# A narrower first kv, fewer z matmuls and another order of copies in a polysketch attention and GELU kernel

## The chip, the cores and the metric

The kernel runs on one core of a Trainium2 chip. The metric is the device time of one execution in microseconds (us). Before the change it is 271.33 us, the median of three runs (270.78 to 271.49). The engines are named as in the profile: PE is TensorE (PEld its weight loads), DVE is VectorE, ACT is ScalarE, POOL is GpSimd, SP is SyncE, which here only starts transfers.

## The reference

Polynomial-sketch attention on 4 batches, 4 heads, 1088 tokens and 32 channels per head, then a two-layer MLP with the exact GELU on the 4352 rows of 128 channels:

```python
def phi(x):                                   # 32 channels -> 64 features
    a = np.einsum('rd,bhsd->bhsr', S1, x)
    b = np.einsum('rd,bhsd->bhsr', S2, x)
    return np.einsum('bhsi,bhsj->bhsij', a, b).reshape(*x.shape[:-1], r * r)
q_p, k_p = (phi(q), phi(k))
kv = np.einsum('bhsf,bhsd->bhfd', k_p, v)     # per head 64 x 32
z = np.sum(k_p, axis=2)                       # per head 64: the features summed over the tokens
num = np.einsum('bhsf,bhfd->bhsd', q_p, kv)
den = np.einsum('bhsf,bhf->bhs', q_p, z)[..., None] + 1e-06
x = num / den                                 # then (B, S, H*D)
h = x @ w_in                                  # 128 -> 2048
g = 0.5 * h * (1.0 + erf(h * inv_sqrt2))
out = g @ w_out                               # 2048 -> 128
```

## The kernel before

Each batch has 8 tokens on each of 128 partitions (the main part, 1024 tokens) and a rest of 64 tokens. Batch 0 is computed alone at the start; later batches' attention is woven into the MLP's products. Tiles that matter: `k_p` holds the main part's features (two tiles per batch, heads of equal parity together), `k_p_rem` those of the rest, `k_s` (the buffers `bits_r`) features added over tokens, `kz` the finished kv and z of a batch.

Batch 0: the features are the stationary operand and v, widened by 32 columns of ones, moves; kv comes out in columns 0 to 31 and z, repeated, in columns 32 to 63.

```python
def kv_first(ps, r, tokens=range(J)):
    for i in tokens:
        ch, t, one = i // 4, i // 2 % 2, i % 2
        for c in range(NP):                   # two heads side by side
            pe.matmul(ps[c * F:(c + 1) * F, r * 2 * D:(r + 1) * 2 * D], lhsT=flat(k_p[0, r][:, t, c * 4 + ch * 2 + one]),
                      rhs=v_aug[r][:, c, i, :], start=(r == 0 and i == 0), stop=False, skip_group_check=True)
# kv_first_rem: the same for the rest, with v_rem_aug[0]
```

Later batches: v or ones is the stationary operand and the features move, four heads side by side. The features of the main part are added over t and over half of what is left, so that two sums per head remain, which go through a product with ones:

```python
def add_tokens(b, r, eng):                    # cut: reshapes
    eng.tensor_add(out=k_s[r], in0=kp[:, 0], in1=kp[:, 1])
    eng.tensor_add(out=k_s[r][:, :, 0], in0=k_s[r][:, :, 0], in1=k_s[r][:, :, 1])

def kv_sum(b, ps):
    for i in range(J):
        ch, t, one = i % 2, i // 4, i // 2 % 2
        for h in range(H):
            kv_product(ps, main["v", b][:, h, i, :], flat(k_p[b, h % 2][:, t, h // 2 * 4 + ch * 2 + one]), b, h, 0, start=i == 0)
    for m in range(2):
        for h in range(H):
            kv_product(ps, ones, k_s[h % 2][:, h // 2, 0, m], b, h, 1)
    for part in range(2):
        for h in range(H):
            kv_product(ps, ones_rem[b // 2] if part else v_rem_aug[b][:, h, :], flat(k_p_rem[b % 2][:, h]), b, h, part, stop=True)
```

Batch 1's `add_tokens` runs on GpSimd, those of batches 2 and 3 on VectorE, right after the features. GpSimd's main work is `token_sums`, four adds or subtractions of 128x512 for each block of four hidden products.

The opening, in the order in which each engine works (cut):

```python
key_turn(0, 0, hidden_bank(), by_act)
keep_busy(1, bank, 128)                       # a product of zeros that fills a gap on TensorE
sketches()
# ... features of batch 0, expand_products(0), kv_first, kv_first_rem
query_turn(1, lambda **a: late.append(a))     # transposes; the copy is kept for later
act.copy(out=kz[0], in_=kv_bank[:, :128])
w_in[0].mantissas(); w_in[0].signs(); w_in[0].product(pool)   # weights from 64-bit words
# ...
w_in[1].low_words()
by_act(**late[0])
w_in[1].fields(); w_in[1].exponents(); w_in[1].mantissas()
for banks, tokens in zip(nd, parts):
    numerators_by_token(0, banks, tokens)
expand_products(1)
for banks, tokens in zip(nd, parts):
    divide(0, banks, tokens, by_head_pair=True)
expand_copy(1, 0)
turn_half(0, 0, hidden_bank(), by_dve)
turn_half(0, 1, hidden_bank(), by_act)
for half in range(2):
    first_hidden(half, range(1))
w_in[1].signs(); w_in[1].product(pool)
expand_copy(1, 1)
```

The instructions of an engine run in the order of the text; what a wait on one of them holds up, it holds up for everything behind it on that engine.

Of the kernel before, what the change touches and what calls it, by code (L numbers as in the profile page):

```python
# [8 lines left out]
FP = mybir.dt.float32  # L9
# [7 lines left out]
def kernel(  # L17
# [18 lines left out]
    pe, dve, act, pool, sp = nc.tensor, nc.vector, nc.scalar, nc.gpsimd, nc.sync  # L36
    B, H, S, D = q.shape
    R = S1.shape[0]
    F = R * R
# [37 lines left out]
    def hidden_bank():  # L77
        return hps.tile([128, CW], FP, name="h_ps")
# [146 lines left out]
    kz_late = big.tile([128, 128], FP, name="kz_late")  # L225

    def rearrange_kz():
        at = [x.rearrange("f (r two d) -> f r two d", r=2, two=2) for x in (kz_late, kz[0])]
        for c in range(NP):
            to, of = (x[c * F:(c + 1) * F] for x in at)  # L230
            for two in range(2):
                pool.tensor_copy(out=to[:, :, two], in_=of[:, :, two if c == 0 else 1 - two])

    ones = big.tile([128, D], FP, name="ones")

    ones_rem = [big.tile([128, D], FP, name=f"ones_rem{i}") for i in range(B // 2)]
    for i, t in enumerate(ones_rem):
        pool.memset(t, 0.0)
        pool.memset(t[i * REM:(i + 1) * REM], 1.0)

    v_rem_aug = [big.tile([128, H, D if b else 2 * D], FP, name=f"v_rem_aug{b}") for b in range(B)]
    pool.memset(v_rem_aug[0], 0.0)
# [2 lines left out]

    v_aug = [att.tile([128, NP, J, 2 * D], FP, name="sums") for r in range(2)]
    for t in v_aug:
        dve.memset(t, 1.0)

    class Rounding:  # L250

# [161 lines left out]
    def add_tokens(b, r, eng):  # L413

        words = mlp.tile([128, LC], U32, name="bits_r")
        k_s[r] = words.bitcast(FP).rearrange("p (c two one f) -> p c two one f", c=NP, two=2, one=2)
        kp = k_p[b, r].rearrange("p t (c two one) i j -> p t c two one (i j)", c=NP, two=2)
        eng.tensor_add(out=k_s[r].rearrange("p c two one f -> p (c two one f)"),
                       in0=kp[:, 0].rearrange("p c two one f -> p (c two one f)"),
                       in1=kp[:, 1].rearrange("p c two one f -> p (c two one f)"))  # L420
        eng.tensor_add(out=k_s[r][:, :, 0], in0=k_s[r][:, :, 0], in1=k_s[r][:, :, 1])

    def flat(features):
        return features.rearrange("p i j -> p (i j)")

    def kv_first(ps, r, tokens=range(J)):

        for i in tokens:

            ch, t, one = i // 4, i // 2 % 2, i % 2  # L430
            for c in range(NP):
                pe.matmul(ps[c * F:(c + 1) * F, r * 2 * D:(r + 1) * 2 * D], lhsT=flat(k_p[0, r][:, t, c * 4 + ch * 2 + one]),  # L432
                          rhs=v_aug[r][:, c, i, :], start=(r == 0 and i == 0), stop=False, skip_group_check=True)

    def kv_first_rem(ps):
        for r in range(2):
            for c in range(NP):
                pe.matmul(ps[c * F:(c + 1) * F, r * 2 * D:(r + 1) * 2 * D], lhsT=flat(k_p_rem[0][:, 2 * c + r]),
                          rhs=v_rem_aug[0][:, 2 * c + r, :], start=False, stop=True, skip_group_check=True)

    def kv_product(ps, lhsT, features, b, h, part, start=False, stop=False):

        at, c = kz_cols(b, h)[part], h // 2
        pe.matmul(ps[at:at + D, c * F:(c + 1) * F], lhsT=lhsT, rhs=features, start=start, stop=stop, skip_group_check=True)  # L444
# [5 lines that stand above are left out]
            for h in range(H):  # L450
                kv_product(ps, main["v", b][:, h, i, :], flat(k_p[b, h % 2][:, t, h // 2 * 4 + ch * 2 + one]), b, h, 0,
                           start=i == 0)
        for m in range(2):
            for h in range(H):
                kv_product(ps, ones, k_s[h % 2][:, h // 2, 0, m], b, h, 1)
        for part in range(2):
            for h in range(H):
                kv_product(ps, ones_rem[b // 2] if part else v_rem_aug[b][:, h, :], flat(k_p_rem[b % 2][:, h]), b, h, part,
                           stop=True)

    kv_T = {}

# [40 lines left out]
    def expand_copy(n, i):  # L503
        A[i] = att.tile([128, 2, CW // 2], FP, name="A_sb")
        act.copy(out=A[i][:, :, :width[n] // 2], in_=B_of[n, i][:, :, :width[n] // 2])  # L505
# [80 lines left out]
    def turn_half(n, i, ps, copy):  # L586
        if i == 0:
            xT[n] = att.tile([128, CW], FP, name="xT", bufs=3)
        for j in range(2):
            pe.transpose(ps[:, j * 128:(j + 1) * 128], in_=x_tok[n, i][:, j].rearrange("p h d -> p (h d)"), identity=ident)  # L590
        copy(out=xT[n][:, i * 256:(i + 1) * 256], in_=ps[:, :256])
# [26 lines left out]
    def first_hidden(half, fis):  # L618

        for fi in fis:  # L620
            if half == 0:
                first_banks[fi] = hidden_bank()
            cols = slice(half * 256, (half + 1) * 256)
            pe.matmul(first_banks[fi][:, cols], lhsT=w_tile(w_in_sb, fi), rhs=xT[0][:, cols], start=True, stop=True)  # L624
# [148 lines left out]
    def keep_busy(n, ps, cols=256):  # L773
        for i in range(n):
            noughts = [nc.const_aps.tensor(0.0, [128, m], FP) for m in (128, cols)]
            pe.matmul(ps[:, CW - cols:], lhsT=noughts[0], rhs=noughts[1], start=True, stop=True)  # L776
# [8 lines left out]
    r.signs()  # L785
    r.product_for_heads(SR_heads)
    key_turn(0, 0, hidden_bank(), by_act)
    keep_busy(1, bank, 128)
    sketches()
    key_turn(0, 1, hidden_bank(), by_act)  # L790
    query_turn(0)
# [19 lines left out]
    w_in[0].exponents()  # L811
    late = []
    query_turn(1, lambda **a: late.append(a))
    act.copy(out=kz[0], in_=kv_bank[:, :128])
    w_in[0].mantissas()
    w_in[0].signs()
    w_in[0].product(pool)
    load_w_out(0, gated=True)
    load_rest()
    w_out = [Rounding(w, beside=b) for w, b in zip(w_out_sb[:2], w_in)]  # L820
    w_in[1].low_words()
    by_act(**late[0])
    w_in[1].fields()
    w_in[1].exponents()
    w_in[1].mantissas()
    parts = [range(2), range(2, JC)]
    nd = [[hidden_bank(), hidden_bank()], [out_bank(), out_bank()]]
    for banks, tokens in zip(nd, parts):
# [1 line left out]
    expand_products(1)  # L830
    for banks, tokens in zip(nd, parts):
        divide(0, banks, tokens, by_head_pair=True)
    expand_copy(1, 0)
    turn_half(0, 0, hidden_bank(), by_dve)
    turn_half(0, 1, hidden_bank(), by_act)
    for half in range(2):
        first_hidden(half, range(1))
    w_in[1].signs()
    w_in[1].product(pool)
    expand_copy(1, 1)  # L840
# [9 lines left out]
    def at(t, f, *a):  # L850
        slots[t].append(lambda: f(*a))
# [19 lines left out]
    def outer_of_all(b, adds_by=dve):  # L871
        for r, a in enumerate(held["factors"]):
            k_p[b, r] = att.tile([128, 2, J, R, R], FP, name="k_p")
            for t in range(2):
                dve.tensor_mul(**spread(k_p[b, r][:, t], a[:, t, :, 0:R], factors(held["keys"][t], r)[:, :, R:2 * R]))
        for r in range(2):
            add_tokens(b, r, adds_by)

    held = {}

# [34 lines left out]
    at(18, expand_products, 2)  # L915
    at(18, query_features, 2, 0)
    at(19, query_features, 2, 1)
    at(21, finish_keys, 1)
    at(22, lambda: turn_kv(1, held["kv"]))
    at(23, query_turn, 3)  # L920
# [54 lines left out]
    for t in range(len(steps) + LAG):  # L975
        if t < 4:

            hidden(0, t)
            if t == 1:
                w_out[0].exponents()  # L980
                w_out[0].low_words()
                w_out[0].finish()
                w_out[1].fields()
            if t == 2:
                w_out[1].low_words()
            if t == 3:
                banks = work_banks()
                numerators_by_token(1, halves(banks), range(JC))
                w_out[1].mantissas(by_pool=True)
                w_out[1].exponents()  # L990
                divide(1, banks, range(JC), by_head_pair=False)
                w_out[1].signs()
                w_out[1].product()
                for u in range(4):
                    for f, *a in products[u]:
                        f(*a)
            continue
        if t == 4:
            for i, copy in enumerate((by_act, by_dve)):
                turn_half(1, i, work_bank(), copy)  # L1000
            for f, *a in products[t]:
                f(*a)
        for n in drains[t]:
            drain(n)
        if t < len(steps):
            n, fi = steps[t]
            hidden(n, fi, by_halves=t >= 18 and (n < NMAIN or fi < 5))
        if t < len(steps) and steps[t][0] < NMAIN and steps[t][1] % NB == NB - 1:
            n, b = steps[t][0], steps[t][1] // NB
            if b >= first_block(n):  # L1010
                token_sums(n, b)
        for f in slots[t]:
            f()
        for n in done[t]:
            store(n)
        if t != 4:
            for f, *a in products[t]:
                f(*a)
# [41 lines left out]
```

## Time and profile before

| | us | share of the span |
|---|---|---|
| time, median of three runs | 271.33 | |
| span of the profiled run | 269.7 | |
| PE busy | 264.9 | 98% |
| PEld busy | 138.8 | 51% |
| DVE busy | 154.3 | 57% |
| ACT busy | 136.6 | 51% |
| POOL busy | 170.2 | 63% |

Lines of the profile name the line of the kernel (L444), the engine, the tile written and the tiles read, the shape, and the count. Times in a timeline are the start and the length, both in us, and then the group. L432 and L438 are batch 0's kv, L444 the later batches' kv and z, L418 and L421 the two adds of `add_tokens`, L561 the numerators by token, L609 the hidden products, L659 to L662 the token sums on GpSimd. A busy PE is not a PE at its peak, since its matmuls overlap.

### The profile page before, as it was taken

The numbers are of one execution on the slowest core, as the hardware profiler recorded it, in microseconds if no ns is written. First come the engines' busy times: TensorE is split into PE (matmuls) and PEld (weight loads), VectorE is DVE, ScalarE is ACT, GpSimd is POOL, SyncE is SP. The second block draws the span as 40 slices with busy tenths as digits, with TensorE's granted clock in tenths as the row PEclk, the third lists the DMA queues.
The fourth block names the chain that finished last, engine by engine and source line by source line (L and its number), as shares of the span: only waits on it lengthen the run. The fifth ranks groups of instructions, "written<-read, shape, count | busy, mean of one in ns | idle before, by whom it ended". The sixth has DMA issues, their size and how long they took to land.

```text
span 269.7 us, 6251 instructions
## 1 busy us (share of the span) xinstructions
PE 264.9 (98%) x2559; PEld 138.8 (51%) x2559; DVE 154.3 (57%) x248; ACT 136.6 (51%) x272; POOL 170.2 (63%) x178
## 2 busy tenths in 40 slices
PE   8999999999999999999999999999999999999994
PEld 6745445354444545445445545444444444445794
DVE  5876878515793699379214996287018901750240
ACT  4664767456635633573347433663357334633431
POOL 3513007899998498468865896668866886777300
PEclk9999999999999999999999999999999999999999
DMA  6479263535201000110200000100200020011020
GB/s 203 125 223 351 56 171 67 160 69 163 47 2 29 12 0 2 23 20 0 41 1 2 0 2 17 24 2 5 36 0 0 2 40 2 0 22 20 1 42 20
DMA packets 37869, 13.52 MB, mean 50 GB/s; under 512 B 28240, under 2 KB 37200, under 8 KB 37840
## 3 DMA queue, kind: packets, MB, share of 16 engines
q1 hardware_dynamic: 37648, 13.05, 19.2%
q8 instruction: 20, 0.33, 0.5%
q10 hardware_dynamic: 192, 0.07, 0.1%
q14 instruction: 9, 0.07, 0.1%
HBM read 10.88 MB, written 2.23 MB: 49 GB/s over the span
## 4 chain that ended last, share of the span: by engine, by line
PE 95%; DVE 3%; ACT 1%; issue 0%; DVEq 0%; ACTq 0%
PE h_ps L609 43%; PE o_ps L694 32%; PE o_ps L745 5%; PE w_ps L498 3%; PE w_ps L742 3%; PE w_ps L538 3%; PE w_ps L444 2%; PE w_ps L776 1%; PE w_ps L375 1%; PE h_ps L333 1%; DVE x_tok L582 1%; DVE bits_m L287 1%; PE o_ps L432 0%; PE h_ps L624 0%; DVE bits_e L292 0%
## 5 line engine op out<-in xcount | busy, mean ns | idle before, releaser
L609 PE MATMUL h_ps<-xT,w_in 128*64 128x512 f32 (+3 forms) x516 | 139.8, 577 | 0.0
L616 ACT ACTIVATE block<-h_ps 128x512 f32<-128x512 f32 (+1 forms) x128 | 72.8, 571 | 101.6 <-PE h_ps L609 98.5
L694 PE MATMUL o_ps<-block,w_out 128*64 128x256 f32 x224 | 57.9, 381 | 0.0
L609 PEld LDWEIGHTS h_ps<-xT,w_in 128*64 128x64 f32 (+1 forms) x516 | 41.8, 143 | 28.6 <-issue 8.6
L659 POOL TENSOR_TENSOR bits_low<-block 128x512 f32<-128x512 f32 x28 | 36.4, 1302 | 27.7 <-ACT block L616 27.6
L694 PEld LDWEIGHTS o_ps<-block,w_out 128*64 128x64 f32 x224 | 30.0, 137 | 36.9 <-issue 27.4
L660 POOL TENSOR_TENSOR bits_a<-block 128x512 f32<-128x512 f32 x28 | 36.0, 1287 | 15.9 <-ACT block L616 15.6
L662 POOL TENSOR_TENSOR bits_m<-block,bits_e 128x512 f32<-128x512 f32 x28 | 36.4, 1298 | 2.2
L661 POOL TENSOR_TENSOR bits_e<-bits_a,block 128x512 f32<-128x512 f32 x28 | 36.2, 1294 | 2.2
L545 DVE RECIPROCAL den<-den 128x512 f32<-128x512 f32 (+1 forms) x7 | 21.9, 3121 | 13.6 <-ACT den L544 13.5
L694 PE MATMUL o_ps<-bits_a,small 128*64 128x256 f32 x112 | 29.0, 382 | 0.0
L694 PE MATMUL o_ps<-bits_m,w_out 128*64 128x256 f32 x112 | 28.8, 380 | 0.0
L694 PE MATMUL o_ps<-bits_low,small 128*64 128x256 f32 x112 | 28.7, 379 | 0.0
L694 PE MATMUL o_ps<-block,small 128*64 128x256 f32 x112 | 28.7, 379 | 0.0
L511 DVE TENSOR_TENSOR q_pT<-A_sb,w_ps 128x512 f32<-128x512 f32 x16 | 10.4, 682 | 30.4 <-ACT A_sb L505 30.3
L710 DVE TENSOR_TENSOR sums<-o_ps,sums 64x512 f32<-64x512 f32 x8 | 5.5, 683 | 35.9 <-ACT sums L707 20.4
L694 PEld LDWEIGHTS o_ps<-block,small 128*64 128x64 f32 x112 | 15.3, 137 | 18.0 <-issue 12.8
L549 DVE TENSOR_TENSOR xT<-w_ps,den 32x512 f32<-32x512 f32 (+1 forms) x28 | 18.2, 649 | 1.0
L694 PE MATMUL o_ps<-bits_e,small 128*64 128x256 f32 x112 | 16.8, 379 | 0.0
L745 PE MATMUL o_ps<-g,w_out 128*128 128x512 f32 x32 | 16.4, 600 | 0.2 <-DVE w_out L297 0.2
L544 ACT ACTIVATE den<-w_ps 32x512 f32<-32x512 f32 (+1 forms) x28 | 15.6, 557 | 1.3 <-PE w_ps L538 1.0
L694 PEld LDWEIGHTS o_ps<-bits_low,small 128*64 128x64 f32 x112 | 15.3, 137 | 0.0
(164 smaller groups left out, 318.5 us busy)
## 6 DMA issues: line engine op xcount, KB each, us to landing
block<-in_moe_w_in_dram SPq DMA_DIRECT2D x3, 512.0 KB, 7.0
block<-in_moe_w_out_dram SPq DMA_DIRECT2D x3, 512.0 KB, 10.2
k<-in_k_dram SPq DMA_DIRECT2D x48, 32.0 KB, 1.8
v<-in_v_dram SPq DMA_DIRECT2D x3, 512.0 KB, 4.3
q<-in_q_dram SPq DMA_DIRECT2D x24, 64.0 KB, 3.5
out_dram<-oT SPq DMA_DIRECT2D x24, 64.0 KB, 2.2
k<-in_k_dram SPq DMA_DIRECT2D x2, 256.0 KB, 2.8
q<-in_q_dram SPq DMA_DIRECT2D x2, 256.0 KB, 4.2
```

The lines of the kernel that those rows point to most:

```text
L511: dve.tensor_mul(out=qp[n].rearrange("f r (g x) -> f g r x", g=G)[:, 2 * i:2 * i + 2], in0=a, in1=b)
L544: act.activation(out=den[h * D:(h + 1) * D, :W], in_=banks[h // 2][at:at + D, :W], func=ACT.Copy, bias=1e-6)
L545: dve.reciprocal(out=den[:, :W], in_=den[:, :W])
L549: dve.tensor_mul(out=xT[n][rows, :W], in0=banks[h // 2][at:at + D, :W], in1=den[rows, :W])
L609: pe.matmul(ps[rows, :W], lhsT=w[:, rows], rhs=xT[n][:, :W], start=True, stop=True)
L616: act.activation(out=g_of[n, fi][:, :W], in_=ps[:, :W], func=ACT.Gelu)
L659: pool.tensor_sub(out=s[3], in0=a11, in1=a21)
L660: pool.tensor_add(out=s[1], in0=a21, in1=a22)
L661: pool.tensor_sub(out=s[2], in0=s[1], in1=a11)
L662: pool.tensor_sub(out=s[4], in0=a12, in1=s[2])
L694: pe.matmul(acc[n][bank][half * 64:(half + 1) * 64, col:col + HW], lhsT=fixed, rhs=moving, start=opens and e == 0 and name in "4715", stop ...
L745: pe.matmul(o_of[n], lhsT=w_tile(w_out_sb, fi), rhs=g, start=first, stop=final)
```

## The change

It makes batch 0's kv from v and a single column of ones (33 moving columns instead of 64), and spreads z only when it is rearranged for later use. For later batches it adds the features over all of a partition's main tokens and, on that batch's 64 partitions, over the rest as well, on VectorE: then one product with ones per head gives z, and the products of the rest with ones and the second half of the sums go away. In the opening it changes the order of some copies and weight steps behind the first numerators, and halves a filler product. The diff, cut to its core (the matching slices in `kv_first_rem` and the smaller memset of `v_aug` are as one expects):

```diff
     def rearrange_kz():
...
+            pool.tensor_copy(out=to[rows, :, c], in_=of[rows, :, 0])
+            pool.tensor_copy(out=to[rows, :, 1 - c], in_=of[rows, :, 1, 0:1].broadcast_to([F, 2, D]))
...
+    def add_last(b, eng):
+        rows = slice(b // 2 * REM, (b // 2 + 1) * REM)
+        for r in range(2):
+            to = k_s[r][:, :, 0, 0]
+            eng.tensor_add(out=to, in0=to, in1=k_s[r][:, :, 0, 1])
+            eng.tensor_add(out=to[rows], in0=to[rows], in1=k_p_rem[b % 2][rows, r::2].rearrange("p c i j -> p c (i j)"))
...
-                pe.matmul(ps[c * F:(c + 1) * F, r * 2 * D:(r + 1) * 2 * D], lhsT=flat(k_p[0, r][:, t, c * 4 + ch * 2 + one]),
-                          rhs=v_aug[r][:, c, i, :], start=(r == 0 and i == 0), stop=False, skip_group_check=True)
+                pe.matmul(ps[c * F:(c + 1) * F, r * 2 * D:r * 2 * D + C], lhsT=flat(k_p[0, r][:, t, c * 4 + ch * 2 + one]),
+                          rhs=v_aug[r][:, c, i, :C], start=(r == 0 and i == 0), stop=False, skip_group_check=True)
...
-        for m in range(2):
-            for h in range(H):
-                kv_product(ps, ones, k_s[h % 2][:, h // 2, 0, m], b, h, 1)
-        for part in range(2):
-            for h in range(H):
-                kv_product(ps, ones_rem[b // 2] if part else v_rem_aug[b][:, h, :], flat(k_p_rem[b % 2][:, h]), b, h, part,
-                           stop=True)
+        for h in range(H):
+            kv_product(ps, v_rem_aug[b][:, h, :], flat(k_p_rem[b % 2][:, h]), b, h, 0, stop=True)
+        for h in range(H):
+            kv_product(ps, ones, k_s[h % 2][:, h // 2, 0, 0], b, h, 1, stop=True)
...
-    keep_busy(1, bank, 128)
+    keep_busy(1, bank, 64)
...
-    act.copy(out=kz[0], in_=kv_bank[:, :128])
+    kz_of, kv_of = (x.rearrange("f (r x) -> f r x", r=2)[:, :, :C] for x in (kz[0], kv_bank[:, :128]))
+    act.copy(out=kz_of, in_=kv_of)
...
+    by_act(**late[0])
     w_in[1].low_words()
-    by_act(**late[0])
     w_in[1].fields()
     w_in[1].exponents()
-    w_in[1].mantissas()
...
-    expand_copy(1, 0)
-    turn_half(0, 0, hidden_bank(), by_dve)
-    turn_half(0, 1, hidden_bank(), by_act)
+    turn_half(0, 0, hidden_bank(), by_act)
+    turn_half(0, 1, hidden_bank(), by_dve)
     for half in range(2):
         first_hidden(half, range(1))
+    expand_copy(1, 0)
+    w_in[1].mantissas()
     w_in[1].signs()
...
+        if adds_by is dve:                    # end of outer_of_all, which makes a batch's features
+            add_last(b, dve)
...
+    at(20, add_last, 1, dve)
     at(21, finish_keys, 1)                    # kv_sum(1)
...
             if t == 1:
+                w_out[0].low_words()
                 w_out[0].exponents()
-                w_out[0].low_words()
```

## The prediction

> **What bounds the kernel now.** I read the chain of work that ended last on the page first, then the chain in order of time over the opening, then each engine's timeline where the change touches it. The page's chain and its first group:
>
> ```profile
> PE 95%; DVE 3%; ACT 1%; issue 0%; DVEq 0%; ACTq 0%
> ...
> L609 PE MATMUL h_ps<-xT,w_in 128*64 128x512 f32 (+3 forms) x516 | 139.8, 577 | 0.0
> ```
>
> TensorE sets the end: what it has to do after the opening, plus every wait in it, is the time. So a matmul taken out of the steady part counts in full, and so does any time for which TensorE is made to wait. The chain in order of time shows the last place at which TensorE waits for another engine:
>
> ```profile
> 22.62 0.41 DVE bits_e L292
> ...
> 23.13 0.44 DVE w_out L297
> 23.56 0.14 issue
> 23.70 1.10 PE o_ps L745 x2
> ```
>
> Ahead of 23.70 us VectorE and ScalarE share the path; behind it TensorE runs without a gap to the end. The change touches both parts.
>
> **How a small matmul is paced.** The TensorE timeline (start, length, group; a float32 matmul leaves two records, except a transpose):
>
> ```profile
> 10.73 1.15 PE L432 MATMUL o_ps<-sums,k_p 128*64 128x64 f32 x32
> 11.81 0.45 PE L438 MATMUL o_ps<-v_rem_aug,k_p_rem 128*64 128x64 f32 x8
> 12.20 0.66 PE L333 MATMUL o_ps<-ident,q 128*128 128x128 f32 x4
> ...
> 20.04 1.14 PE L561 MATMUL w_ps<-kz,q_pT 64*64 64x33 f32 x64
> 21.11 1.98 PE L745 MATMUL o_ps<-g,w_out 128*128 128x512 f32 x4
> ```
>
> I use starts only. L432 and L438 put two heads side by side in the array, so 32 records are 16 pairs of records and 8 are 4. From 10.73 to 11.81 is 1.08 us, from 11.81 to 12.20 is 0.39: twelve pairs are 0.69, 58 ns for a pair, with 0.15 per change of group. L561 runs four tiles at once: 64 records are 16 quads in 1.07 us, and less 0.15 that is again 58 ns. L432 moves 64 columns, L561 only 33; what they share is a stationary operand 64 columns wide.
>
> **What the Trainium skill says.** Its page "TensorE: Matmul & The Clock Gate", section "LDWEIGHTS (loading the stationary operand)", puts a weight load at the columns of the stationary operand divided by 1.2, in ns. For 64 that is an estimate of 53 ns, near the 58 seen in both groups: the trace agrees that the load paces them. The page "SBUF — State Buffer", section "Who interferes with whom", says that a VectorE instruction with two SBUF inputs and a GpSimd instruction that reads SBUF exclude each other, and that the loser waits for the winner's whole instruction. The trace agrees, and this decides my number:
>
> ```profile
> 98.45 1.27 POOL L661 TENSOR_TENSOR bits_e<-bits_a,block 128x512 f32<-128x512 f32 x1
> 98.92 1.35 DVE L418 TENSOR_TENSOR bits_r<-k_p 128x512 f32<-128x512 f32 x1
> ...
> 99.80 1.61 POOL L662 TENSOR_TENSOR bits_m<-block,bits_e 128x512 f32<-128x512 f32 x1
> ...
> 100.31 1.38 DVE L421 TENSOR_TENSOR bits_r<-bits_r 128x256 f32<-128x256 f32 x1
> ...
> 101.61 0.68 DVE L418 TENSOR_TENSOR bits_r<-k_p 128x512 f32<-128x512 f32 x1
> ...
> 102.32 1.38 DVE L421 TENSOR_TENSOR bits_r<-bits_r 128x256 f32<-128x256 f32 x1
> ...
> 103.55 1.29 POOL L660 TENSOR_TENSOR bits_a<-block 128x512 f32<-128x512 f32 x1
> 103.63 0.70 DVE L484 STREAM_TRANSPOSE qT<-q 128x512 f32<-128x512 f32 x1
> 104.05 0.94 PEld L444 LDWEIGHTS w_ps<-k_p,v 128*32 128x32 f32 x64 [0.81 <-DVE bits_r L421]
> ...
> 104.97 0.41 PE L444 MATMUL w_ps<-bits_r,ones 128*32 128x64 f32 x16
> ```
>
> This is batch 2's feature sum. An L418 add with no GpSimd instruction in its way takes 0.68 us; L421 has half its elements and takes 1.38 each time, because it starts inside a GpSimd instruction of 1.3 us and finishes 0.28 after it. The two engines take turns. And the sums are ready at 103.70 for matmuls that want them at 104.97: only 1.3 us of slack.
>
> **Part by part.**
> Batch 0's narrower kv: 36 matmuls go from 64 to 33 moving columns. Their stationary operand stays 64 wide, so by the pair pace above nothing is saved. If the columns set the pace, a pair of records would fall to 33/64 of 58 ns, 28 ns less, and the 36 pairs (72 records) would give 1.0 us.
> The filler before the sketches: half its columns. Its two records stand 0.21 us apart before the clock has risen; 0.1 to 0.2 goes, on the path. I take 0.2.
> Order behind the first numerators: VectorE's mantissa product (13.44, 0.43 long) leaves the place ahead of the first division, which can start about 0.3 earlier; but the first half's copy, now on ScalarE, starts only after the transpose at the end of the expansion, so about 0.1 of it reaches the first hidden product. Further on, the low words move ahead of the exponents (0.4 us on ScalarE); yet the division for the second chunk waits for its numerators, which TensorE's order holds (20.04 to 21.11). I pass on 0.1 and no more. Opening: −0.3 us.
> Fewer matmuls in later batches: 48 per batch become 40. Four heads run side by side, and the row of 16 records of the ones product, 55.21 to 55.43 in batch 1, is four quads: 56 ns each. Eight matmuls are 16 records, four quads, 0.22 us; three batches, −0.67 us.
> The new adds: per batch four more VectorE adds, two pairs, the second of each pair depending on the first. All have two SBUF inputs. Unhindered a pair is under 0.5 us (an estimate from L418's 0.68 for 512 elements). But they are the last thing before the ones product, which now comes last of the sum, and GpSimd is busy with token sums of 1.27 to 1.34 us, four in a row.
> Batch 2, in turns: GpSimd's L660 holds until 104.84; first add, done 105.05; L661 until 106.25; second add, 106.45; L662 until 107.66; third and fourth, 108.1. The ones product would be due at 105.08, after the main products (0.92) and the four of the rest (0.11). TensorE stands for 3.0 us.
> Batch 3: the previous L421 ends at 162.57, GpSimd's next starts at 162.68. The first add slips in, the other three each wait for one GpSimd instruction: 167.0 against 164.2 due. 2.8 us.
> Batch 1: the adds come behind L511 at 54.35; GpSimd starts a row of four at 54.40. One add before it, three behind one instruction each: 58.9 against 55.3. 3.6 us.
> Sum of the waits: 9.4 us. Nothing behind them can take it back, as TensorE has no other gap. 271.33 − 0.3 − 0.67 + 9.4 = 279.8 us.
>
> **The rivals.**
> (a) The adds fit in. The intention of the change: fewer matmuls, and VectorE, busy 57% of the span, takes the work. The share speaks for it; the slack of 1.3 us in batch 2 against four taking-turns adds speaks against it. It would make 270.4 us.
> (b) Half of the waiting. If an add that waits for nothing follows its predecessor before GpSimd gets its turn, one GpSimd instruction of about 1.3 us falls out of each batch: 9.4 − 3.9 = 5.5, that is 275.9 us. Against it: at 159.39 an L418 that followed an L421 without a wait still took 1.76 us behind GpSimd's L662.
> (c) The columns do set the pace in batch 0: 1.0 us less than any of these. L561's 58 ns with 33 columns speaks against it.
> (d) More waiting: in batch 1 the GpSimd row starts within 0.05 us of the first add; if it wins, one more turn, +1.3: 281.
>
> **Range and chances.** The centre is the turn-by-turn count, 279.8. The low end is rival (b), 275.9, the high end (d) with a little on top, 281.8. The 2% line above the time before is 276.8, so slower by over 2% needs about 6.4 us of waiting: two thirds of my count. I give 0.8 to slower, 0.19 to the same (rival (a) and the low part of (b)), 0.01 to faster.
>
> **What would show it.** Right: the ones product waiting for VectorE's new adds in the waits, some 3 us in each of three batches; adds of 1.3 us mean where their elements would take 0.2 to 0.3; L432's successor still at 58 ns for a pair; TensorE's steady part beginning near 23.4. Wrong: ones products directly behind the rest's products with no idle time (then (a)), or a batch 0 sum half as long (then (c)). It would be most wrong if an add this small passed between GpSimd instructions without taking turns, or if the adds stood earlier in VectorE's queue than the trace of before lets me place them.

## The result, and the profile after

The changed kernel takes 282.33 us, the median of six executions (280.53 to 282.6), against 271.1 us before (270.78 to 271.5): a ratio of 1.0395, with a 95% interval of 1.036 to 1.0429. It is slower by 11.2 us, where 8.5 were predicted, and the time lies half a microsecond above the predicted range.

The page of the changed kernel, in its order: busy time of the engines, the clock granted to TensorE in 40 slices of 7 us, the chain that ended last, the costliest group.

```profile
PE 267.5 (95%) x2511; PEld 139.1 (50%) x2511; DVE 159.8 (57%) x260; ACT 136.4 (49%) x272; POOL 169.4 (60%) x174
...
PEclk9999999979999999799999999999999999999999
...
PE 79%; DVE 15%; ACT 3%; DMA 2%; issue 1%; SPq 0%; DVEq 0%
...
L609 PE MATMUL h_ps<-xT,w_in 128*64 128x512 f32 (+3 forms) x516 | 142.4, 588 | 0.0
```

VectorE's share of the chain has gone from 3% to 15%, so TensorE now waits for it somewhere in the steady part. The group of the hidden products, which the change doesn't touch, has gone from 139.8 to 142.4 us for the same 516 records. And the clock row has two slices at 7, the ninth and the seventeenth, that is around 60 and 115 us. The last two are not among the prediction's signs.

The waits of the changed kernel between 23 and 270 us (engine, tile and line, what it waited for; microseconds in all, times, longest):

```profile
ACT kv_T L465 <- PE w_ps L447: 10.7, 3, 3.8
...
PE w_ps L447 <- DVE bits_r L424: 7.7, 5, 2.3
...
PEld w_ps L447 <- DVE bits_r L424: 5.3, 3, 2.5
```

TensorE's ones product (L447) waits for the second new add (L424), in three batches, as predicted. Batch 2 in order of time, all engines (start, length, engine and line; L423 is the first add of a pair, L424 the second, L659 to L662 are GpSimd's token sums in the MLP):

```profile
107.55 1.30 POOL L660 TENSOR_TENSOR bits_a<-block 128x512 f32<-128x512 f32 x1
107.64 1.37 DVE L423 TENSOR_TENSOR bits_r<-bits_r 128x128 f32<-128x128 f32 x1
...
108.05 1.10 PE L447 MATMUL w_ps<-k_p,v 128*32 128x64 f32 x64
...
108.93 1.26 POOL L661 TENSOR_TENSOR bits_e<-bits_a,block 128x512 f32<-128x512 f32 x1
108.97 0.29 PE L447 MATMUL w_ps<-k_p_rem,v_rem_aug 128*32 128x64 f32 x8
109.04 1.31 DVE L424 TENSOR_TENSOR bits_r<-bits_r,k_p_rem 64x128 f32<-64x128 f32 x1
110.28 1.26 POOL L662 TENSOR_TENSOR bits_m<-block,bits_e 128x512 f32<-128x512 f32 x1
110.38 1.31 DVE L423 TENSOR_TENSOR bits_r<-bits_r 128x128 f32<-128x128 f32 x1
...
110.40 0.30 PE L447 MATMUL w_ps<-bits_r,ones 128*32 128x64 f32 x2 [1.14 <-DVE bits_r L424]
111.72 0.29 DVE L424 TENSOR_TENSOR bits_r<-bits_r,k_p_rem 64x128 f32<-64x128 f32 x1
...
112.06 0.31 PE L447 MATMUL w_ps<-bits_r,ones 128*32 128x64 f32 x6 [1.37 <-DVE bits_r L424]
...
112.31 0.43 PE L694 MATMUL o_ps<-block,w_out 128*64 128x256 f32 x1
```

Three adds in a row begin some 0.1 us after a GpSimd instruction has begun and end 0.15 us after it has ended (107.64 + 1.37 = 109.01 for 107.55 + 1.30 = 108.85); the fourth meets none and takes 0.29. TensorE does its main products at 108.05 and those of the rest at 108.97, and then stands until 112.06, but for two of the eight records of the ones product at 110.40, for which the first pair of adds is enough. That is the turn-by-turn count of the prediction. What it lacks is what comes next. The same kernel in stretches around the waits of batches 1 and 2 (stretch and its length; busy time and instructions of PE, PEld, DVE, ACT and POOL; the granted clock; DMA share and GB/s):

```profile
54.40:58.30 3.90, 1.01 (x30) 0.63 (x20) 3.87 (x4) 0.10 (x1) 3.74 (x4) 1.00 0.22 48
58.30:61.70 3.40, 3.40 (x12) 1.16 (x10) 0.01 (x1) 0.91 (x3) 1.68 (x2) 0.50 0.31 70
61.70:65.10 3.40, 3.40 (x28) 1.28 (x26) 0.00 (x0) 1.19 (x2) 2.54 (x3) 1.00 0.74 196
108.90:112.90 4.00, 1.50 (x42) 0.93 (x32) 3.87 (x6) 0.27 (x1) 2.53 (x2) 1.00 0.01 4
112.90:116.30 3.40, 3.40 (x18) 1.63 (x16) 1.98 (x4) 0.75 (x2) 0.00 (x0) 0.50 0.04 8
116.30:119.70 3.40, 3.40 (x51) 1.68 (x50) 0.12 (x1) 1.33 (x3) 1.10 (x1) 1.00 0.23 36
```

The second row of each three is the new thing: TensorE is busy again for all of it, but at half the clock, and gets 12 matmuls done where the stretch after it does 28, and 18 where the stretch after it does 51 (the products aren't the same ones, but the direction is plain). The page "TensorE: Matmul & The Clock Gate" of the Trainium skill, section "What's actually happening", says that the clock falls to half after an idle window of about 3.4 us. The trace agrees on the half, 0.50, and each of the two lasts 3.41 us. At half the clock such a stretch does 1.7 us less work. TensorE wasn't wholly idle ahead of it, though.

How idle it was can be read. The clock of this trace changes at 3.67, 58.28, 61.70, 112.90 and 116.31 us, and these times lie 16, 1, 15 and 1 times 3.413 us apart. So they belong to a row of stretches of that length. The two stretches that end where the clock falls, and the two across which batch 3's wait lies (172.91 to 175.55):

```profile
54.87:58.28 3.41, 0.72 (x10) 0.52 (x12) 3.38 (x4) 0.09 (x1) 3.25 (x4) 1.00 0.20 45
...
109.49:112.90 3.41, 1.13 (x14) 0.73 (x16) 3.31 (x5) 0.27 (x1) 1.97 (x2) 1.00 0.02 5
...
170.92:174.34 3.42, 2.05 (x78) 1.16 (x74) 3.32 (x5) 0.75 (x2) 3.03 (x3) 1.00 0.00 0
174.34:177.75 3.41, 2.44 (x24) 1.43 (x26) 3.06 (x5) 0.47 (x2) 0.77 (x1) 1.00 0.00 0
```

The clock fell behind 0.72 and 1.13 us of work and did not fall behind 2.05 and 2.44. From the clock's rise to the end of the kernel, the traces of all thirteen kernels have no exception to this: it fell behind every stretch with up to 1.46 us of TensorE work (e10_alike_dependent, 109.68 to 113.09) and behind none with 1.69 or more (e1_adds_left_out, 263.29 to 266.71). Of these runs, e1 leaves the adds out and e10 changes one of them; both are described below. By this, batch 3's wait cost no clock because it lies across two stretches: within one it would have left at most 0.8 us of work there, an estimate from 3.41 less 2.64.

Where the stretches lie differs between executions. Two of the six of the changed kernel, 280.53 and 280.65 us, have a mean clock of 0.992 and 0.993 in place of 0.987, which fits one half-clock stretch and not two; they left no trace, and a third, 282.41 us at 0.992, doesn't fit.

**Where 10.9 us came from**, in the profiled executions (269.67 before, 280.56 after). The waits are measured as the start of the first product behind the sum, less the time at which it was due, which is the start of the sum plus the work in it:

| Part | Predicted | Measured |
|---|---|---|
| Opening, until the product with `w_out` at 23.70 before, 22.87 after | −0.3 | −0.83 |
| 8 fewer matmuls in each of three sums | −0.67 | −0.67 (worked out) |
| Wait in batch 1 (58.08 for 54.72) | 3.6 | 3.36 |
| Wait in batch 2 (112.31 for 109.31) | 3.0 | 3.00 |
| Wait in batch 3 (175.55 for 172.91) | 2.8 | 2.64 |
| Two stretches of 3.41 us at half the clock | none | +3.4 |
| Sum | +8.4 | +10.9 |

The value for the fewer matmuls is the worked-out one, and the sum of the rest leaves room for it; the others are read from the trace. A run below bears it out: in e7_two_adds batch 3's sum has 4 matmuls fewer and no wait, and takes 1.37 us (162.72 to 164.09) against 1.48 before (163.18 to 164.66).

### The profile page after: what moved, and what is told of

Its sections match the earlier page's. It is cut to its first block, busy times and chain, and to the rows that moved or that the text cites. A ratio compares the mean times of both kernels' runs of the same rounds, so it can differ in the third digit from the quotient of the medians.

```text
span 280.6 us, 6162 instructions
## 1 busy us (share of the span) xinstructions
PE 267.5 (95%) x2511; PEld 139.1 (50%) x2511; DVE 159.8 (57%) x260; ACT 136.4 (49%) x272; POOL 169.4 (60%) x174
## 3 DMA queue, kind: packets, MB, share of 16 engines
HBM read 10.88 MB, written 2.23 MB: 47 GB/s over the span
## 4 chain that ended last, share of the span: by engine, by line
PE 79%; DVE 15%; ACT 3%; DMA 2%; issue 1%; SPq 0%; DVEq 0%
PE h_ps L609 36%; PE o_ps L694 25%; PE o_ps L745 5%; PE w_ps L498 3%; PE w_ps L742 3%; DVE bits_r L424 2%; PE w_ps L538 2%; DVE den L545 2%; DVE bits_r L423 2%; DVE bits_r L416 2%; DVE xT L549 2%; DVE k_p L876 2%; ACT den L544 2%; DMA q<-in_q_dram 2%; DVE bits_r L413 2%; PE w_ps L370 1%
## 5 line engine op out<-in xcount | busy, mean ns | idle before, releaser
L609 PE MATMUL h_ps<-xT,w_in 128*64 128x512 f32 (+3 forms) x516 | 142.4, 588 | 0.0
L659 POOL TENSOR_TENSOR bits_low<-block 128x512 f32<-128x512 f32 x28 | 36.1, 1290 | 38.4 <-ACT block L616 38.3
L662 POOL TENSOR_TENSOR bits_m<-block,bits_e 128x512 f32<-128x512 f32 x28 | 36.2, 1291 | 2.2
```

The source lines that it names most:

```text
L609: pe.matmul(ps[rows, :W], lhsT=w[:, rows], rhs=xT[n][:, :W], start=True, stop=True)
L659: pool.tensor_sub(out=s[3], in0=a11, in1=a21)
L662: pool.tensor_sub(out=s[4], in0=a12, in1=s[2])
```

## The experiments

The theory: the loss is the new adds taking turns with GpSimd, plus the clock that falls behind the two longest of the waits. Rivals: the opening or the shorter filler lost something too; the clock fell for another reason; the adds are slow by themselves and not for GpSimd.

### The adds left out, and the adds alone

**e1_adds_left_out**: the changed kernel, with the sums of later batches as before (48 matmuls); the narrow kv, the order and the filler stay changed.

```diff
-        if adds_by is dve:
-            add_last(b, dve)
...
-    at(20, add_last, 1, dve)
 # kv_sum again with two ones products and ones_rem
```

> The changed kernel with the later batches' sums as before (two ones products of the main part and the one of the rest, no new adds); batch 0's narrow kv and the new order stay. Theory (the new adds take turns with GpSimd and hold TensorE, and the clock falls in the holes): no waits in the three sums, clock 1.00, 269.9 to 270.9 us, that is the opening's gain of some 0.3 to 0.8 alone. Rival (the opening's order or the rearranged kz cost time as well): above 272 us.

Measured: 270.81 us (270.31 to 272.56), before 270.95; ratio 1.0002 [0.9987, 1.0018]. No wait for the new adds and a clock of 1.000, and from the product with `w_out` to the end the profile has 245.97 us, as before. The whole loss is in the adds, and all the rest of the change together makes no difference that these runs can show.

**e2_adds_alone**: the kernel before, with only `add_last` and the shorter sum.

```diff
+    def add_last(b, eng): ...            # as in the change
...
+        if adds_by is dve:
+            add_last(b, dve)
...
+    at(20, add_last, 1, dve)
 # kv_sum with 40 matmuls, as in the change
```

> The kernel before with the new adds and the shorter sum alone. Theory: the same three waits of 2.6 to 3.4 us and one or two half-clock stretches of 3.4 us: 281 to 284 us. Rival (the adds are late only because the opening and the order shifted the engines against each other): below 276 us.

Measured: 281.93 us (280.91 to 283.51), ratio 1.0411 [1.0369, 1.0454]. TensorE's waits for the second add are 7.7 and 5.3 us, the same two numbers as in the changed kernel, and the clock is at half from 58.45 to 61.87 and from 113.07 to 116.48 us. Both parts of the loss come from the adds.

### The clock by itself

**e3_filler**: the changed kernel with five products of zeros, 2.4 us of TensorE by the trace (54.79 to 57.16 in batch 1), ahead of the ones product, into columns that nothing reads. The adds are as late as before, but TensorE is busy for most of the wait.

```diff
         for h in range(H):
             kv_product(ps, v_rem_aug[b][:, h, :], flat(k_p_rem[b % 2][:, h]), b, h, 0, stop=True)
+        keep_busy(5, ps)
```

> The changed kernel with five products of zeros (some 2.1 us of TensorE) ahead of the ones product of each sum, so that TensorE is busy for most of the wait. Theory (two half-clock stretches of 3.4 us cost 1.7 us each): clock 1.00 in the middle of the run, 278.5 to 279.6 us, with the adds as long as before. Rival (the clock readings are a by-product, the waits alone make the time): 281.5 us or more.

Measured: 279.05 us (278.07 to 279.19), ratio 1.0292 [1.0274, 1.031]. Span and mean clock of its profile:

```profile
core 0: 277.4 us, clock 1.000
```

Against 280.6 us at 0.987. The three sums last as long as in the changed kernel, from the first product of each to the first behind it: 4.62, 4.25 and 3.90 us here, 4.62, 4.26 and 3.90 there. Both kernels from the end of their openings: 257.69 us after, 254.31 here. The difference, 3.38 us, is the clock's alone, and twice 1.7 is 3.4. So work that computes nothing made the kernel 3.3 us faster, and the missing term of the prediction is measured. (Without the clock, 279.05 lies within 0.8 of the predicted 279.8.)

### What the adds wait for

**e4_one_input**: the second add of `add_tokens` and the first of each pair become one reduction over the tokens, which reads one operand from SBUF. The rest's add goes; its ones product is back on TensorE, 44 matmuls in a sum.

```diff
-            add_last(b, dve)
...
+            z_s[r] = att.tile([128, NP, F], FP, name="z_s")
+            dve.tensor_reduce(out=z_s[r], in_=k_s[r].rearrange("p c two one f -> p c f (two one)"),
+                              axis=mybir.AxisListType.X, op=AX.add)
 # batch 1: of k_s[r][:, :, 0], GpSimd having done the second add
```

> The changed kernel with the second half of the sum over tokens as one VectorE reduction per head pair, which reads a single SBUF tensor; the rest's ones product goes back to TensorE (44 matmuls per batch, not 40 or 48). Theory (two SBUF inputs make the turns): each reduction takes its own time only (0.3 to 0.7 us), the ones product doesn't wait, 269.6 to 270.6 us. Rival (anything on VectorE at this place comes late, whatever its inputs): reductions of over 1.2 us and waits of over 1 us per batch, above 273 us.

Measured: 270.53 us (270.11 to 272.18), ratio 0.9989 [0.9973, 1.0005], and no wait. Batch 2:

```profile
102.69 1.28 POOL L675 TENSOR_TENSOR bits_low<-block 128x512 f32<-128x512 f32 x1 [0.43 <-ACT block L632]
102.73 2.02 DVE L429 TENSOR_REDUCE z_s<-bits_r 128x128 f32<-128x512 f32 x2
...
104.91 1.10 PE L461 MATMUL w_ps<-k_p,v 128*32 128x64 f32 x64
...
105.82 0.29 PE L461 MATMUL w_ps<-z_s,ones 128*32 128x64 f32 x8
```

Both reductions begin within a GpSimd instruction and end when their own work is done, 1.05 us for one (0.42 in batch 1, of half as many elements); the ones product follows the main products without a gap. That VectorE is slow by itself falls: a reduction reads 512 elements on each partition, where an L423 reads twice 128, and takes less time. It is the second input. The Trainium skill, "SBUF — State Buffer", section "Who interferes with whom", says that a VectorE instruction with at most one SBUF input, outside its two-port modes, doesn't contend with GpSimd, and that on this chip `tensor_reduce` never does; this trace agrees, with 1.05 us for each reduction of batch 2.

**e5_one_input_filler128** is e4 with the opening's filler at its old width. It asks whether the shorter filler makes the clock rise late in some executions.

```diff
-    keep_busy(1, bank, 64)
+    keep_busy(1, bank, 128)
```

> The kernel with one VectorE reduction in place of the adds, and the filler before the sketches back at 128 columns. Theory (the shorter filler leaves TensorE less busy while its clock is still to rise, and in some executions it rises a whole stretch later): no execution above 271.5 us, median 270.2 to 270.6. Rival (the executions at 272 us come from elsewhere): one in five stays near 272 us, median as with the short filler, 270.5 us.

Measured: 270.48 us (269.92 to 276.25), ratio 0.9975 [0.9958, 0.9991]: the one version that beats the kernel before by more than the measurement is uncertain, by a quarter of a per cent; as one of ten intervals it may be chance. A single execution at 272.97 contradicts what I had expected of the filler. (Executions more than 1.5% above the fastest of their kernel, such as 276.25 here and 276.7 in e7, are left out of the ratios and stay unexplained.)

### Adds that need nothing of each other

**e7_two_adds**: the changed kernel without the rest's add. Two adds are left in each batch, and neither needs the other.

```diff
             eng.tensor_add(out=to, in0=to, in1=k_s[r][:, :, 0, 1])
-            eng.tensor_add(out=to[rows], in0=to[rows], in1=k_p_rem[b % 2][rows, r::2]...)
 # and the rest's product with ones_rem back
```

> The changed kernel with only the first of the two new adds of each head pair (L423, 128 partitions, not dependent on each other); the rest's ones product is back on TensorE. Theory (each add waits for one GpSimd instruction of 1.3 us when one stands ready): waits of about 0.5, 1.2 and 0 us in the three batches, no half-clock stretch, 272 to 273 us. Rival (the wait is set by the dependent add of 64 partitions or by the rest's features): no wait, 270.3 us.

Measured: 271.0 us (270.62 to 276.7), ratio 0.9995 [0.9975, 1.0014]. Waits of 0.5 and 1.2 us had been expected in batches 1 and 2; measured as in the table they are 0.56 and 0.07. The second is a miss, and so is the time (272 to 273), for this reason (batch 2):

```profile
103.13 1.29 POOL L667 TENSOR_TENSOR bits_a<-block 128x512 f32<-128x512 f32 x1
103.21 1.57 DVE L429 TENSOR_TENSOR bits_r<-bits_r 128x128 f32<-128x128 f32 x2
...
104.50 1.41 POOL L668 TENSOR_TENSOR bits_e<-bits_a,block 128x512 f32<-128x512 f32 x1
...
104.78 0.36 PE L452 MATMUL w_ps<-bits_r,ones 128*32 128x64 f32 x8
```

Two adds take 1.57 us together: one turn for both, and GpSimd's next instruction takes 1.41 instead of 1.27, as it waited for the second. So not every add pays for a turn.

**e9_adds_in_two_pairs** uses that: the four adds of the changed kernel, with the two firsts ahead of the two seconds. Nothing else differs.

```diff
+        to = [k_s[r][:, :, 0, 0] for r in range(2)]
         for r in range(2):
-            to = k_s[r][:, :, 0, 0]
-            eng.tensor_add(out=to, in0=to, in1=k_s[r][:, :, 0, 1])
-            eng.tensor_add(out=to[rows], in0=to[rows], in1=k_p_rem[b % 2][rows, r::2]...)
+            eng.tensor_add(out=to[r], in0=to[r], in1=k_s[r][:, :, 0, 1])
+        for r in range(2):
+            eng.tensor_add(out=to[r][rows], in0=to[r][rows], in1=k_p_rem[b % 2][rows, r::2]...)
```

> The changed kernel with the same four adds in another order: both heads pairs' first adds, then both dependent ones. Theory as mended by the run with two adds (a turn is lost where an add waits for the one before it; adds that don't depend on each other pass together): about 2.1, 1.6 and 0.1 us of waiting in the three batches, 3.8 in all instead of 9, and no half-clock stretch: 273 to 274.5 us. Rival (every add with two SBUF inputs loses a turn, in whatever order): as the changed kernel, 280 us or more.

Measured: 274.31 us (273.88 to 274.78), ratio 1.0116 [1.0099, 1.0133], clock 1.000, and waits, measured as in the table, of 2.23, 1.68 and 0.32 us: 4.2 in all, where 3.8 had been expected. The time is as expected. The order of four small adds gives back 8 of the 11 us: 4.8 of waiting (9.0 less 4.2) and the clock's 3.4, 8.2 together. Batch 2:

```profile
104.89 1.31 POOL L661 TENSOR_TENSOR bits_a<-block 128x512 f32<-128x512 f32 x1
104.99 1.57 DVE L423 TENSOR_TENSOR bits_r<-bits_r 128x128 f32<-128x128 f32 x2
...
106.28 1.40 POOL L662 TENSOR_TENSOR bits_e<-bits_a,block 128x512 f32<-128x512 f32 x1
...
106.59 1.44 DVE L425 TENSOR_TENSOR bits_r<-bits_r,k_p_rem 64x128 f32<-64x128 f32 x2
...
107.89 0.52 PE L448 MATMUL w_ps<-bits_r,ones 128*32 128x64 f32 x8 [1.28 <-DVE bits_r L425]
```

Two turns, one for each pair, where the changed kernel has three. My reading after this was that an add loses its turn if it depends on the one ahead of it. But the changed kernel speaks against that: its third add (L423 at 110.38) needs nothing of the second and lost one all the same. Two more runs asked what decides.

**e10_alike_dependent**: the rest's add becomes a second add of the main part over all rows, so that all four adds have one shape and each pair is still a chain. The sum leaves the rest's features out and counts a quarter of the main part twice.

```diff
-            eng.tensor_add(out=to[rows], in0=to[rows], in1=k_p_rem[b % 2][rows, r::2]...)
+            eng.tensor_add(out=to, in0=to, in1=k_s[r][:, :, 1, 0])
```

> The changed kernel with the rest's add (64 rows) replaced by one more add of the main part over all 128 rows: each pair's second add still depends on its first, but all four adds now have one shape. The rest's features are left out of the sum and a quarter of the main part is counted twice. It asks what lets two adds pass GpSimd together: in the changed kernel the third add (first of the second pair) needs nothing of the second and still loses a turn in all three batches. Theory that likeness of shape lets them pass: the third add starts some 0.08 us before the second ends and passes with it in batches 1 and 3, one turn of 1.3 us less in each, and batch 1's TensorE wait too short for the clock to fall: about 278 us. Theory that an add which follows one that depended on its predecessor loses its turn whatever its shape: three turns per batch as before, the third add at 1.3 us, 282 to 283 us with two half-clock stretches.

Measured: 281.0 and 276.78 us in two executions, too far apart to choose between the two expected times. The first is the profiled one, with the two half-clock stretches; the second has a clock of 1.000 and no trace. Batch 2:

```profile
108.99 1.26 POOL L661 TENSOR_TENSOR bits_e<-bits_a,block 128x512 f32<-128x512 f32 x1
109.09 1.31 DVE L424 TENSOR_TENSOR bits_r<-bits_r 128x128 f32<-128x128 f32 x1
...
110.33 0.28 DVE L423 TENSOR_TENSOR bits_r<-bits_r 128x128 f32<-128x128 f32 x1
...
110.33 1.39 POOL L662 TENSOR_TENSOR bits_m<-block,bits_e 128x512 f32<-128x512 f32 x1
```

The third add passes, 0.28 us, behind a second that depended on the first; in batch 3 too, and in batch 1 it doesn't (it begins at 55.08, GpSimd's instruction at 54.97). Both theories fall: the third add of batch 2 passes though the one ahead of it depended on its own predecessor, and that of batch 1, with the same shapes, doesn't.

**e11_unlike_independent**: e7 with the second add cut to half of its rows; half of that sum is left out.

```diff
+            part = slice(0, 128 - 64 * r)
-            eng.tensor_add(out=to, in0=to, in1=k_s[r][:, :, 0, 1])
+            eng.tensor_add(out=to[part], in0=to[part], in1=k_s[r][part, :, 0, 1])
```

> The version with only the two independent adds, the second of them cut to 64 of its 128 rows (the other half of that sum is left out), so that the two adds differ in shape but neither needs the other. Theory that likeness of shape lets two adds pass together: the second loses a turn in batch 2, where its like passed in 0.28 us, the ones product comes 1.2 us late there, 272.2 us. Theory that lack of dependence does it: the two pass together in batches 2 and 3 as before, 1.57 and some 0.5 us for two, no more wait than the version with whole adds, 271.0 us.

Measured: 270.94 us (270.74 to 272.8), ratio 1.0002 [0.9981, 1.0023]. The pair in batch 2:

```profile
103.04 1.57 DVE L430 TENSOR_TENSOR bits_r<-bits_r 128x128 f32<-128x128 f32 x2
...
104.34 1.41 POOL L669 TENSOR_TENSOR bits_e<-bits_a,block 128x512 f32<-128x512 f32 x1
```

Unlike shapes pass together as well, so likeness falls here a second time. What agrees with every add of these kernels' traces is simpler: who comes up first. In e10's batch 2 the add and GpSimd's instruction begin together, at 110.33, and the add passes; in the changed kernel GpSimd's begins at 110.28 and the add at 110.38, and it loses; in e10's batch 1 it is 0.11 us behind and loses; the second add of a pair, which waits for its first, is some 0.1 us behind in batches 2 and 3 and loses, 109.09 for 108.99. The section of the Trainium skill named above says that the order of issue decides who blocks, not the shape of the operation; these starts agree. Dependence seems to matter only as far as it makes the add 0.1 us late; no run moves an add's start alone. The changed kernel's third add, which depends on nothing ahead of it, starts 0.03 us after the end of the second in batches 2 and 3, where the second covers partitions 64 to 127. It starts 0.07 before that end in batch 1 (55.01 for 55.08), where the second covers partitions 0 to 63, and 0.08 before it in e10, where it covers all. So the number of rows isn't what makes it late; where they start goes with it, and no run varies that alone.

### The opening

**e6_filler64_alone**: the kernel before with the filler at 64 columns.

```diff
-    keep_busy(1, bank, 128)
+    keep_busy(1, bank, 64)
```

> The kernel before with the filler of 64 columns alone. Theory (late clock): the median moves by no more than 0.2 us, but some executions stand about 1.5 us above the others, which the kernel before doesn't show (270.6 to 271.5). Rival (the filler only takes its own 0.1 to 0.2 us away, as predicted): all executions 0.1 to 0.2 us faster.

Measured: 270.9 us (270.6 to 272.74), ratio 0.9996 [0.9981, 1.0012]. One execution at 272.74, but the kernel before has 5 of 56 at 272.75 and more. That the shorter filler makes some executions late falls; the filler makes no difference that can be measured.

**e8_opening_filler128**: e1 with the old filler, so the narrow kv and the order of copies alone.

```diff
-    keep_busy(1, bank, 64)
+    keep_busy(1, bank, 128)
```

> The changed kernel without the new adds and with the filler at 128 columns: the narrow kv and the order of copies alone. Theory (at the same rise of the clock the order is worth 0.1 to 0.25 us and the narrow kv nothing): 270.6 to 270.9 us, no execution near 272 us. Rival (the narrow kv is worth up to 1 us): 269.9 us.

Measured: 270.65 us (270.35 to 272.51), before 271.22; ratio 0.9994 [0.9983, 1.0006], with three executions from 271.9 to 272.5, where none had been expected near 272. A gain of 1 us from the narrow kv, 0.9963, is outside the interval. The changed kernel's trace says the same (batch 0, 33 columns):

```profile
10.09 1.12 PE L435 MATMUL o_ps<-sums,k_p 128*64 128x33 f32 x32
11.16 0.43 PE L441 MATMUL o_ps<-v_rem_aug,k_p_rem 128*64 128x33 f32 x8
```

From 10.09 to 11.16 is 1.07 us for the 32 records, against 1.08 with 64 columns. Half the moving columns save nothing.

## Why the prediction failed, by its own steps

**The step that failed is the sum itself**: "Nothing behind them can take it back, as TensorE has no other gap. 271.33 − 0.3 − 0.67 + 9.4 = 279.8 us." It takes a wait to cost its own length. Two of the three cost 1.7 us more, since the clock fell to half for 3.41 us behind them. That term is 3.4 us (e3: 3.38), and with it the same sum gives 283.2, against 282.33: in the profile the opening is 0.5 shorter than was said, and the waits are 0.4 shorter. The range, whose high end was rival (d) "with a little on top", had no room for it.

**The adds' waits, +9.4: right.** Measured 3.36, 3.00 and 2.64, 9.0 together. The tile's instructions in the changed kernel (count: shortest, median and longest in ns; first and last start in us) show the turns:

```profile
L423 DVE TENSOR_TENSOR bits_r<-bits_r x6: 279/1308/1368, 53.5 to 172.6; 128x128 f32<-128x128 f32 x6
...
L424 DVE TENSOR_TENSOR bits_r<-bits_r,k_p_rem x6: 290/1304/1314, 53.8 to 173.9; 64x128 f32<-64x128 f32 x6
```

0.28 us unhindered, 1.3 in the median: four of the six of the first kind and five of the second pay for a GpSimd instruction.

**Rival (b), half of the waiting: wrong here, but half true.** It said that "an add that waits for nothing follows its predecessor before GpSimd gets its turn". In the changed kernel none of the third adds did. In e7, e9 and e11 the second of two adds did in batches 2 and 3, and in e10 the third. It wanted the start of the add compared with the start of GpSimd's next instruction to 0.1 us, which the trace before allowed for other adds and not for these. **Rival (a), the adds fit in:** wrong for two inputs; with one input (e4) it is what happens, at 270.53 us against its 270.4. **Rival (d)** didn't come: batch 1's first add began at 53.51 us, ahead of GpSimd's first at 53.58.

**Fewer matmuls, −0.67:** nothing contradicts it, and the sum closes with it. But 0.22 us for each batch was bought with waits of 2.6 to 3.4.

**The narrow kv, 0: right**, and rival (c) falls: 1.07 us for 1.08, and e8.

**The opening, −0.3: can't be told.** The profile has −0.83, but the clock rose at 3.67 us in that execution and at 6.63 in the one before. That doesn't follow the filler: over all profiled kernels it rose between 3.67 and 9.87 us with 64 columns, and between 3.84 and 6.63 with 128. From the first numerators to the steady part, where the rise is past, it is 10.92 us before (and in e6), 10.76 after, 10.77 in e8 and 10.87 in e1: 0.05 to 0.16 for the order, where 0.1 was said. In the times, e1, e6 and e8 all have 1 in their interval.

## What to carry to other kernels

Ahead of moving small work to VectorE beside a busy GpSimd, ask how many SBUF inputs each instruction has and count GpSimd instructions, not elements; where two inputs can't be avoided, put adds that need nothing of each other in a row (here 282.3 to 274.3 us), or sum with one reduction of one input (270.5). To a TensorE wait of about 3 us add what the clock may cost behind it, 1.7 us here, and look for that in the clock row before another cause is sought; some work within the wait can save it (e3). A gain of a few tenths in an opening is smaller than what the clock's rise varies between executions, so it is read from the trace behind the rise, and not from the times.

## What the runs showed of the hardware

The clock's changes lie whole multiples of 3.413 us apart. After its rise it fell behind each such stretch with up to 1.46 us of TensorE work and behind none with 1.69 or more, for 3.41 us at a time where work went on. So the same wait can cost 1.7 us or nothing, by where it lies: the changed kernel's 3.36 and 3.00 us cost it, its 2.64 and e9's 2.23 did not. TensorE's busy times are rough, as its ends are modelled. Of two VectorE adds with two inputs beside GpSimd, the second goes through in 0.28 us if it comes up no later than GpSimd's next instruction, and takes 1.3 if it comes 0.1 us after it. With a stationary operand of 64 columns, a pair of records side by side takes some 58 ns whether 33 or 64 columns move.
